# Turning all four quarters of the keys first, and letting a unit's scores accumulate in one bank

## The chip, the cores and the metric

The kernel runs on one core of one Trainium2 chip. A core has a matrix engine (TensorE, PE in the profile, with its weight loads as PEld), a vector engine (VectorE, DVE), a scalar engine (ScalarE, ACT), a general engine (GpSimd, POOL), a queue processor that here issues the large transfers (SyncE, SP), and 16 DMA engines that move data between the device's memory and the on-chip memory. The metric is the time of one execution on the device, in microseconds (us); less is better.

## What is computed

One decoding step of a windowed attention, gated by a small mixer, with residual:

```
xn = layernorm(x)                                    # x: 2 x 1 x 512
q  = (xn @ wq) as 32 heads of 128
k, v = the last 4096 positions of k_cache, v_cache   # 2 batches, 8 key heads
scores = q . k * 128**-0.5                           # 4 query heads share a key head
s  = (softmax(scores) @ v) as one row of 4096 @ wo
g  = silu(gmlp(xn, w_in, w_sp, b_sp, w_out))
out = x + s * g                                      # everything is float32
```

There is one query row for each batch and head, so nearly all of the work is reading: 16 windows of keys and 16 of values of 4096 x 128 numbers each, and the weights.

## The kernel before, in words

**Units.** The attention is cut into 8 units. A unit is one batch and two neighbouring key heads, so it has 8192 keys; units 0 to 3 are the first batch, 4 to 7 the second. The keys of a unit are one transfer of 4 MB that lays 64 keys (of 128 numbers) on each of the 128 partitions, and its values are another.

**The ring.** All large transfers go through `ring`, four slots of 4 MB each. `enqueue` gives each load the next slot in turn, and `advance` sends the loads, in the order in which they were enqueued, once the program has passed the place where their slot is given up. The loads are: `wq` (two slots), `w_in`, `w_out`, then keys and values by turns (k0, k1, v0, k2, v1, ... k7, v6, v7), and at the end `wo` in three slots: 16 blocks of its rows, then 8, then 4 and four single ones. They all stand in one queue of SP, and a load waits there for whoever still reads its slot.

**Order.** Every engine call passes through `InOrder`, so each engine runs its instructions in the order of the program text; the loop over the units near the end of the kernel sets it.

**Scores of a unit.** The product needs the head dimension on the partitions, so `turn(u, m)` (DVE) turns a quarter of the unit's keys, 16 keys of each partition, in blocks of 32 x 32 into `kt`. `shares(u, m)` then makes four products on PE, one for each quarter `dq` of the head dimension. The weights are the query, 128 x 32, laid out so that the rows of different groups of 32 partitions stay apart; each product writes 32 rows of one PSUM bank, `sh`. These are only shares: the four `dq` have still to be added. ACT copies the bank to `shs`, and `add_shares(u, m)`, a 128 x 128 product with zeros and ones (`add_dq`), adds them and puts them in the rows of bank `s` that belong to quarter `m`. So a unit has 16 products into `sh`, four copies and four products into `s`.

**Softmax and values of a unit.** `share_max` (DVE and one small product into `mo`) finds the maximum over a unit's keys and from it the shift `nb`; `probs` (ACT) takes the exponential of `s` with that shift into `p`; `probs_t` turns it into `pT` (DVE); `values` makes 16 products of `pT` with the unit's values into the bank `acc`, where each writes 32 rows, four row groups in turn; `scale_out` (ACT) keeps the wanted parts as `o`; `collect` adds `o` into the bank `col`, in which all units of a batch meet. `weigh` makes one over the sums of the exponentials, `wd`, at the last unit of a batch. These steps of unit u-1 stand inside unit u's loop step.

**End.** `gather`, `scale_out(last)`, `divide` and `collect_last` make the row `oT`, which the output product needs: 28 blocks of `wo` go into the bank `part`, which ACT copies to `parts`; the last four go into `so`, where the four row groups of `parts` are added to them. Two DVE instructions with the gate and x follow, and the output's transfer.

Of the kernel before, what the change touches and what calls it, by code (L numbers as in the profile page):

```python
# [9 lines left out]
F32 = mybir.dt.float32  # L10
AF = mybir.ActivationFunctionType
ALU = mybir.AluOpType
AX = mybir.AxisListType

P = 128
HQ, DH = 32, 128
G = 4
# [4 lines left out]
def ap(t, offset, dims):  # L22

    return bass.AP(tensor=t.tensor, offset=t.offset + offset, ap=[list(t.ap[0])] + [list(d) for d in dims])
# [18 lines left out]
def kernel(  # L43
# [13 lines left out]
    nc = tc.nc  # L57
    pe, dve, act, sp = (InOrder(tc, e) for e in (nc.tensor, nc.vector, nc.scalar, nc.sync))
    B, _, D = x.shape
    _, HKV, SK, _ = k_cache.shape  # L60
    W = min(4096, max(256, SK // 4))
    REP = HQ // HKV
# [8 lines left out]
    JC = 512 // 32  # L71
    NCH = J // JC
    SLOT = J * DH
    BANKS = {"s": 2, "sh": 2, "acc": 2, "mo": 1, "col": 1}

    cst = ctx.enter_context(tc.tile_pool(name="cst", bufs=1))
# [15 lines left out]
    def advance(*slots):  # L92
        for n in slots:
            free[n] = True
        while queue and all(free[n] for n in queue[0][1]):
            load, at = queue.pop(0)
            for n in at:
                free[n] = False
            load(ring[:, at[0] * SLOT : (at[-1] + 1) * SLOT], at[0])

    def const(name, *shape):
        return cst.tile([P, *shape], F32, tag=name, name=name)

    def bank(name, tag):
        return ps.tile([P, 512], F32, tag=tag, name=name, bufs=BANKS[tag])

# [33 lines left out]
    units = []  # L140
    for n in range(NU):
        u = Unit()
        u.n, u.kt, u.shs, u.slot = n, {}, {}, {}
        u.b, u.w = divmod(n, NU // B)
        units.append(u)

# [34 lines left out]
    nc.gpsimd.memset(hT, 0.0)  # L181
    x4 = const("x4", DC)
    nc.gpsimd.memset(x4, 0.0)
    add_dq = const("add_dq", NCH - 1 + P)
    nc.gpsimd.memset(add_dq, 0.0)
    sel = const("sel", 56)
    nc.gpsimd.memset(sel, 0.0)
    sel4 = const("sel4", 3 + 32)
# [62 lines left out]
    nc.gpsimd.tensor_mul(perm, ap(rowm, 0, [[1, 32], [0, G]]), ap(grpm, 0, [[0, 32], [1, G]]))  # L251
    perm = perm.rearrange("p h e -> p (h e)")
    for a in range(2):
        nc.gpsimd.tensor_copy(
            ap(add_dq, NCH - 1 + 16 * a, [[32, G], [4, REP]]),
            rowm[:, 16 * a : 16 * a + 16].rearrange("p (g h) -> p g h", g=G),
        )
    am = const("am", 2)
    dve.tensor_reduce(am, rowm.rearrange("p (a x) -> p a x", a=2), axis=AX.X, op=ALU.add)
    negm = const("negm", 2)  # L260
# [14 lines left out]
                    start=(k == 0), stop=(k == KT - 1),  # L275
                )
    advance(0, 1)
    qT = sb.tile([P, 1024], F32, tag="qT", name="qT", bufs=1)
    for r in range(2):
        dve.transpose(qT[:, 512 * r : 512 * r + 512], pq[r])  # L280
    qm = const("qm", 2 * B * 64)
# [12 lines left out]
    def q_of(u, dq):  # L294
        return ap(qbd, (u.n * 4 + dq) * 32, [[1, 32]])
# [52 lines left out]
    def spread_quarters(dst, shares, start=True, stop=True):  # L348
        for g in range(G):
            pe.matmul(  # L350
                dst[32 * g : 32 * g + 32, :], rowm, shares[:, g * DC : (g + 1) * DC], start=start, stop=stop,
            )
# [3 lines left out]
        g = j % G  # L356
        pe.matmul(yp[32 * g : 32 * g + 32, :], hT[:, j, :], wout[:, j, :], start=(j < G), stop=(j >= FT - G))
    advance(3)
    ys = sb.tile([P, D], F32, tag="shs", name="ys")
    act.activation(ys, yp, AF.Copy)  # L360
    y = bank("yq", "mo")[:, :DC]
    spread_quarters(y, ys)
    gate = const("gate", DC)
    dve.tensor_scalar(gate, y, -1.0, 80.0, op0=ALU.mult, op1=ALU.min)
    act.activation(gate, gate, AF.Exp)
    dve.tensor_scalar_add(gate, gate, 1.0)
    dve.reciprocal(gate, gate)
    dve.tensor_mul(gate, gate, y)


    def turn(u, m):

        u.kt[m] = sb.tile([P, JC, DH], F32, tag="kt", name=f"kt{u.n}_{m}", bufs=3)
        dve.transpose(
            u.kt[m].rearrange("p j d -> p (j d)"), u.k[:, JC * m : JC * m + JC, :].rearrange("p j d -> p (j d)")
        )

    def shares(u, m):

        u.sh = bank(f"sh{u.n}_{m}", "sh")  # L380
        for dq in range(4):
            pe.matmul(
                u.sh[32 * dq : 32 * dq + 32, :], q_of(u, dq), u.kt[m][:, :, 32 * dq : 32 * dq + 32],
                start=True, stop=True,
            )
        u.shs[m] = sb.tile([P, 512], F32, tag="shs", name=f"shs{u.n}_{m}")
        act.activation(u.shs[m], u.sh, AF.Copy)

    def add_shares(u, m):

        if m == 0:
            u.s = bank(f"s{u.n}", "s")
        pe.matmul(u.s, add_dq[:, NCH - 1 - m : NCH - 1 - m + P], u.shs[m], start=(m == 0), stop=(m == NCH - 1))

    def share_max(u):
        m2 = sb.tile([P, 2], F32, tag="m2", name=f"m2_{u.n}")
        dve.tensor_reduce(m2, ap(u.s, 0, [[1, 2], [2, 256]]), axis=AX.X, op=ALU.max)
        mg = sb.tile([P, 2, G * NCH], F32, tag="mg", name=f"mg{u.n}")
        dve.tensor_mul(mg, ap(m2, 0, [[1, 2], [0, G * NCH]]), spot.rearrange("p a g m -> p a (g m)"))
        u.mo = bank(f"mo{u.n}", "mo")  # L400
        dve.tensor_add(mg[:, 0], mg[:, 0], mg[:, 1])
        pe.matmul(u.mo[:, : G * NCH], same_r, mg[:, 0], start=True, stop=True)
        mx = sb.tile([P, 1], F32, tag="mx", name=f"mx{u.n}")
        dve.reduce_max(mx, u.mo[:, : G * NCH], axis=AX.X)
        u.nb = sb.tile([P, 2], F32, tag="nb", name=f"nb{u.n}")
        dve.scalar_tensor_tensor(u.nb, ap(mx, 0, [[0, 2]]), -SCALE, negm, op0=ALU.mult, op1=ALU.add)
# [3 lines left out]
    def probs(u):  # L410

        u.p = sb.tile([P, 512], F32, tag="p", name=f"p{u.n}")
        if u.w == 0:
            sums[u.b] = sb.tile([P, NU // B, 2], F32, tag="l", name=f"l{u.b}")
        for a in range(2):
            act.activation(
                ap(u.p, a, [[2, 256]]), ap(u.s, a, [[2, 256]]), AF.Exp,
                bias=u.nb[:, a : a + 1], scale=SCALE, accum_out=sums[u.b][:, u.w, a : a + 1],
            )
# [13 lines left out]
        pe.matmul(u.mo[:, 32:33], lr.rearrange("p w r e -> p (w r e)"), ones[:, 0:1], start=True, stop=True)  # L433
        dve.reciprocal(wd[:, u.b : u.b + 1], u.mo[:, 32:33])

    def values(u, part=0, parts=1):
        if part == 0:
            u.acc = bank(f"acc{u.n}", "acc")
        n = JC // parts
        for j in range(n * part, n * part + n):  # L440
            c = j % G
            pe.matmul(
                u.acc[32 * c : 32 * c + 32, :], u.pT[:, j, :], u.v[:, j : J : JC, :],
                start=(j < G), stop=(j >= JC - G),
            )

    def scale_out(u):
        u.o = sb.tile([P, 4, DH], F32, tag="o", name=f"o{u.n}")
        for jj in range(4):
            o, acc, m = u.o[:, jj, :], u.acc[:, jj * DH : (jj + 1) * DH], diag[:, jj : jj + 1]  # L450
            if u is units[-1] and jj >= 2:
                dve.tensor_scalar_mul(o, acc, m)
            else:
                act.activation(o, acc, AF.Copy, scale=m)
# [13 lines left out]
    def gather(b):  # L468

        hq = sb.tile([P, 32], F32, tag="hq", name=f"hq{b}")  # L470
        by_d = col[0][32 * b : 32 * b + 32, :].rearrange("p (j d) -> p d j", j=NCH)
        for e in range(4):
            dve.reduce_sum(hq[32 * e : 32 * e + 32, :], by_d[:, 32 * e : 32 * e + 32, :], axis=AX.X)
        t = bank(f"oT{b}", "acc")[:, :32]
        pe.matmul(t, perm, hq, start=True, stop=True)
        return t

    def divide(b, t, r=slice(0, P)):
        dve.tensor_scalar_mul(oT[r, :, 16 * b], t, wd[r, b : b + 1])
# [8 lines left out]
        dve.reduce_sum(ol[r, :], t.rearrange("p (j n) -> p n j", j=NCH), axis=AX.X)  # L488
        divide(u.b, ol[r, :], r)

    prev = old = None
    last = units[-1]
    for u in units:
        turn(u, 0)
        shares(u, 0)
        if old is not None and old.n == NU // B - 1:
            divide(0, gather(0))
        if prev is not None:
            share_max(prev)
            probs(prev)  # L500
        turn(u, 1)
        shares(u, 1)
        add_shares(u, 0)
        if prev is not None:
            probs_t(prev)
            weigh(prev)
            if u is not last:
                values(prev)
        for m in range(2, NCH):
            turn(u, m)  # L510
            shares(u, m)
            add_shares(u, m - 1)
        if u is not last and prev is not None:
            scale_out(prev)
        advance(u.slot["k"])
        add_shares(u, NCH - 1)
        if u is not last and prev is not None:
            advance(prev.slot["v"])
            collect(prev)
        old, prev = prev, u  # L520
    values(old, 0, 2)
    share_max(last)
    probs(last)
    values(old, 1, 2)
    advance(old.slot["v"])
    probs_t(last)
    weigh(last)
    scale_out(old)
    values(last, 0, 2)
    collect(old, old.w)  # L530
    early = slice(0, 32 * last.w)
    values(last, 1, 2)
    t = gather(last.b)
    scale_out(last)
    divide(last.b, t[early, :], early)
    collect_last(last)
# [4 lines left out]
    for n in range(EARLY):  # L541
        t, a = blocks[n]
        g = n % G
        pe.matmul(part[32 * g : 32 * g + 32, :], oT[:, n, :], t[:, a, :], start=(n < G), stop=(n >= EARLY - G))
    parts = sb.tile([P, D], F32, tag="shs", name="parts")
    act.activation(parts, part, AF.Copy)
    so = bank("so", "mo")[:, :DC]
    for n in range(EARLY, 32):
# [40 lines left out]
```

## Time and profile before

| | us |
|---|---|
| time, median of 3 runs | 217.53 |
| the three runs | 217.3, 217.53, 218.38 |
| span of the profiled execution, first to last instruction | 215.6 |
| PE busy | 144.9 (67%) |
| DVE busy | 107.1 (50%) |
| ACT busy | 43.7 (20%) |
| read from the device's memory | 89.40 MB, 415 GB/s over the span |

The profile is of one execution, and its span leaves out what lies around the first and last instruction: the median of the three runs is 1.93 us longer than the span. Times inside the span count from its start. A row of the timeline reads: start, duration, engine, line, operation, what is written and read, how many instructions are merged in it; and in brackets the engine's idle time ahead of it with what ended that. Nearly all rows name line 37, the helper that records every call, so the names of the tiles tell them apart. A float32 product shows as two instructions, so 16 products are x32.

### The profile page before, as it was taken

To read this page: it belongs to the slowest core of one execution; us is meant where nothing else is said; L and a number is where in the kernel's file an instruction comes from. 1 tells how busy PE (TensorE), PEld (TensorE's weight loads), DVE (VectorE), ACT (ScalarE), POOL (GpSimd) and SP (SyncE) were. 2 spreads that over 40 slices of the span, in tenths; PEclk is the share of its full clock that TensorE was granted. 3 is DMA by queue.
4 is the path that set the end of the run, shared out by engine and by line. 5 is a ranking of instruction groups with operands and counts; after the bars stand their busy time and mean duration, and the time that the engine had idled before them with its cause. 6 is when DMAs were issued, how large, how long until landed. Compare 5 with 4: busy or idle time off the path is not lost.

```text
span 215.6 us, 2181 instructions
## 1 busy us (share of the span) xinstructions
PE 144.9 (67%) x848; PEld 40.3 (19%) x848; DVE 107.1 (50%) x161; ACT 43.7 (20%) x108; POOL 4.2 (2%) x22
## 2 busy tenths in 40 slices
PE   0010787224595897699599499459949967987663
PEld 0010222100021222122122132112202211222311
DVE  1140025633995943953936663793585089233101
ACT  2030000331124115114303304130331231241001
POOL 6010000000000000000000000000000000000000
PEclk9999999658599699699799789859975996999998
DMA  9898999999999999999999999999999999999990
GB/s 389 390 389 389 431 423 459 435 438 421 450 395 474 395 453 419 444 432 425 439 404 450 419 444 429 432 432 419 444 413 447 425 432 444 425 435 404 410 376 33
DMA packets 3788, 89.52 MB, mean 415 GB/s; under 512 B 434, under 2 KB 450, under 8 KB 964
## 3 DMA queue, kind: packets, MB, share of 16 engines
q1 hardware_dynamic: 3772, 89.40, 96.9%
q8 instruction: 6, 0.10, 0.2%
q14 instruction: 2, 0.02, 0.0%
q10 hardware_dynamic: 8, 0.00, 0.0%
HBM read 89.40 MB, written 0.00 MB: 415 GB/s over the span
## 4 chain that ended last, share of the span: by engine, by line
DMA 41%; PE 39%; DVE 16%; ACT 2%; issue 2%; DVEq 0%
DMA ring<-in_A_wo_dram 20%; PE sh L37 11%; DMA ring<-in_A_k_cache_dram 11%; DVE kt L37 10%; DMA ring<-in_A_wq_dram 10%; PE s L37 10%; PE acc L37 7%; PE q_ps L37 4%; PE y L37 2%; PE z L37 1%; PE col L37 1%; PE mo L37 1%; DVE gate L37 1%; DVE u L37 1%; DVE qm L37 1%
## 5 line engine op out<-in xcount | busy, mean ns | idle before, releaser
L37 DVE STREAM_TRANSPOSE kt<-ring 128x2048 f32<-128x2048 f32 x32 | 72.2, 2286 | 24.9 <-DMA ring<-in_A_k_cache_dram 24.9
L37 PE MATMUL sh<-kt,qbd 128*32 128x512 f32 x256 | 43.6, 725 | 27.0 <-DVE kt L37 27.0
L37 ACT ACTIVATE shs<-sh 128x512 f32<-128x512 f32 x32 | 19.1, 597 | 99.4 <-PE sh L37 99.4
L37 PE MATMUL s<-shs,add_dq 128*128 128x512 f32 x64 | 39.0, 716 | 0.0
L37 PE MATMUL acc<-ring,pT 128*32 128x512 f32 x256 | 31.3, 614 | 0.0
L37 PEld LDWEIGHTS s<-shs,add_dq 128*128 128x128 f32 x64 | 11.0, 215 | 30.9 <-issue 26.5
L37 PEld LDWEIGHTS sh<-kt,qbd 128*32 128x32 f32 x256 | 7.0, 117 | 46.3 <-issue 38.3
L37 PE MATMUL q_ps<-ring,xnT 128*32 128x512 f32 x64 | 8.8, 713 | 7.6 <-DMA ring<-in_A_wq_dram 7.6
L37 PEld LDWEIGHTS acc<-ring,pT 128*32 128x32 f32 x256 | 7.8, 112 | 22.3 <-issue 17.6
L37 DVE TENSOR_REDUCE m<-s 128x2 f32<-128x512 f32 x8 | 5.4, 680 | 13.0 <-PE s L37 12.9
L37 PE MATMUL xnT_ps<-ident,xn 2*128 2x2 f32 x4 | 0.6, 252 | 14.5 <-DVE xn L37 14.5
L37 ACT ACTIVATE o<-acc,diag 128x128 f32<-128x128 f32 x30 | 8.6, 374 | 4.9 <-PE acc L37 4.9
L37 PE MATMUL part<-ring,oT 128*32 128x512 f32 x56 | 6.6, 597 | 3.5 <-DMA ring<-in_A_wo_dram 3.5
L37 ACT ACTIVATE p<-s,nb 128x256 f32<-128x256 f32 x16 | 7.6, 488 | 6.6 <-DVE nb L37 6.4
L37 DVE STREAM_TRANSPOSE qT<-q_ps 128x512 f32<-128x512 f32 x2 | 1.4, 717 | 14.4 <-PE q_ps L37 14.3
L37 PE MATMUL col<-o,sel 128*32 128x512 f32 x14 | 7.3, 601 | 0.0
L37 DVE TENSOR_TENSOR res<-so,gate 128x128 f32<-128x128 f32 x1 | 0.3, 292 | 11.5 <-PE so L37 11.5
L37 DVE STREAM_TRANSPOSE pT<-p 128x512 f32<-128x512 f32 x8 | 5.4, 674 | 1.2 <-ACT p L37 1.2
L37 PE MATMUL y<-ring,hT 128*32 128x512 f32 x14 | 3.3, 996 | 3.8 <-DVE hT L37 3.8
L37 ACT ACTIVATE zs<-z 128x448 f32<-128x448 f32 x1 | 0.5, 544 | 24.7 <-PE z L37 24.7
L37 ACT ACT_TABLE_LOAD x4 | 5.1, 1283 | 0.8 <-PEq L575 0.7
L37 PEld LDWEIGHTS q_ps<-ring,xnT 128*32 128x32 f32 x64 | 2.5, 130 | 13.1 <-issue 13.1
(114 smaller groups left out, 62.2 us busy)
## 6 DMA issues: line engine op xcount, KB each, us to landing
ring<-in_A_k_cache_dram SPq DMA_DIRECT2D x8, 4096.0 KB, 20.0
ring<-in_A_v_cache_dram SPq DMA_DIRECT2D x8, 4096.0 KB, 28.1
ring<-in_A_wo_dram SPq DMA_DIRECT2D x1, 4096.0 KB, 33.2
ring<-in_B_w_in_dram SPq DMA_DIRECT2D x1, 3584.0 KB, 17.1
ring<-in_A_wo_dram SPq DMA_DIRECT2D x1, 2048.0 KB
ring<-in_B_w_out_dram SPq DMA_DIRECT2D x1, 1792.0 KB, 21.0
ring<-in_A_wo_dram SPq DMA_DIRECT2D x1, 1024.0 KB
ring<-in_A_wo_dram SPq DMA_DIRECT2D x4, 256.0 KB, 17.6
```

Source lines behind the costliest of these rows:

```text
L37: return self.tc.keep_in_program_order(call(*args, **kwargs))
```

## The change

- A unit's four quarters are all turned before its scores are made; `kt` has five buffers in place of three, so that four stand ready.
- `scores` makes the same 16 products, now with the quarter `m` choosing the 32 rows and the four `dq` accumulating on them in PSUM. One copy to `shs` and one product with a permutation, `regroup`, put the rows in order. A unit has one copy and one 128 x 128 product where it had four of each.
- `share_max` is split: the maximum of the sums after the second turn, the shift (`shift`) and the exponentials after the third.
- `values` of the unit before stands behind the unit's scores: four products, then the permuting product, then twelve. `scale_out` and `collect` follow. This now holds for unit 7's loop step too, where before the values of unit 6 stood partly behind unit 7's maximum.
- The gate's last steps on DVE stand behind the second turn of unit 0. `yq` is one product and four copies of ACT in place of four products.

```diff
-    def shares(u, m):
-        u.sh = bank(f"sh{u.n}_{m}", "sh")
+    def scores(u):
+        u.sh = bank(f"sh{u.n}", "sh")
         for dq in range(4):
...
+            for m in range(NCH):
+                pe.matmul(
+                    u.sh[32 * m : 32 * m + 32, :], q_of(u, dq), u.kt[m][:, :, 32 * dq : 32 * dq + 32],
+                    start=(dq == 0), stop=(dq == 3),
+                )
+        u.shs = sb.tile([P, 512], F32, tag="shs", name=f"shs{u.n}", bufs=1)
+        act.activation(u.shs, u.sh, AF.Copy)
+    def by_group_of_keys(u):
+        u.s = bank(f"s{u.n}", "s")
+        pe.matmul(u.s, regroup, u.shs, start=True, stop=True)
...
     for u in units:
         turn(u, 0)
-        shares(u, 0)
...
+        turn(u, 1)
         if prev is not None:
             share_max(prev)
+        else:
+            form_gate()
+        turn(u, 2)
+        if prev is not None:
+            shift(prev)
             probs(prev)
...
+        turn(u, 3)
+        advance(u.slot["k"])
         if prev is not None:
             probs_t(prev)
             weigh(prev)
...
+        scores(u)
+        if prev is not None:
+            values(prev, range(G))
+        by_group_of_keys(u)
+        if prev is not None:
+            values(prev, range(G, JC))
             scale_out(prev)
...
+            collect(prev, prev.w if u is last else NU // B - 1)
+        prev = u
-    values(old, 0, 2)
     share_max(last)
+    shift(last)
     probs(last)
-    values(old, 1, 2)
-    advance(old.slot["v"])
     probs_t(last)
     weigh(last)
-    scale_out(old)
-    values(last, 0, 2)
-    collect(old, old.w)
     early = slice(0, 32 * last.w)
-    values(last, 1, 2)
+    values(last, range(8))
     t = gather(last.b)
+    values(last, range(8, JC))
     scale_out(last)
```

The first place is the end of unit 7 on PE. Before, from its last quarter's products on (`sh_3_882` and `s_866` are unit 7's scores, `acc_892` unit 6's values, `acc_941` unit 7's, `mo_905` its maximum and then its sums):

```order
L37 MATMUL sh_3_882<-kt_3_880,qbd 32x512 x4
L37 MATMUL s_866<-shs_2_877,add_dq 128x512
L37 MATMUL s_866<-shs_3_887,add_dq 128x512
L37 MATMUL acc_892<-ring,pT_868 32x512 x8
L37 MATMUL mo_905<-mg_903,same_r 128x16
L37 MATMUL acc_892<-ring,pT_868 32x512 x8
L37 MATMUL mo_905<-ones,lr_932 128x1
L37 MATMUL acc_941<-ring,pT_928 32x512 x8
L37 MATMUL col<-o_936,sel 32x512
L37 MATMUL acc_941<-ring,pT_928 32x512 x8
L37 MATMUL oT_964<-hq_959,perm 128x32
L37 MATMUL ol<-o_966,sel_89 32x128 x4
```

Now, from the last of the 16 score products on (`sh_776`, `s_800`: unit 7's scores; `acc_795`: unit 6's values; `acc_847`: unit 7's):

```order
L37 MATMUL sh_776<-kt_3_771,qbd 32x512
L37 MATMUL acc_795<-ring,pT_774 32x512 x4
L37 MATMUL s_800<-shs_793,regroup 128x512
L37 MATMUL acc_795<-ring,pT_774 32x512 x12
L37 MATMUL col<-o_814,sel 32x512
L37 MATMUL mo_829<-mg_827,same_r 128x16
L37 MATMUL mo_829<-ones,lr_843 128x1
L37 MATMUL acc_847<-ring,pT_839 32x512 x8
L37 MATMUL oT_861<-hq_856,perm 128x32
L37 MATMUL acc_847<-ring,pT_839 32x512 x8
L37 MATMUL ol<-o_871,sel_88 32x128 x4
```

The two small products into `mo` now follow each other with nothing between, all of unit 6's values and its `col` stand ahead of them, and the gathering product stands between the halves of unit 7's values.

The second place is DVE in unit 7, from its first turn to the maximum of its own scores. Before (`s_782` and `pT_868` are unit 6's):

```order
L37 STREAM_TRANSPOSE kt_0_834<-ring 128x2048
L37 TENSOR_REDUCE m_6_843<-s_782 128x2
L37 TENSOR_TENSOR mg_845<-m_6_843,spot 128x32
L37 TENSOR_TENSOR mg_845<-mg_845 128x16
L37 TENSOR_REDUCE mx_850<-mo_847 128x1
L37 SCALAR_TENSOR_TENSOR nb_852<-mx_850,negm 128x2
L37 STREAM_TRANSPOSE kt_1_857<-ring 128x2048
L37 STREAM_TRANSPOSE pT_868<-p_854 128x512
L37 STREAM_TRANSPOSE kt_2_870<-ring 128x2048
L37 STREAM_TRANSPOSE kt_3_880<-ring 128x2048
L37 TENSOR_REDUCE m_7_901<-s_866 128x2
```

Now (`s_728` and `pT_774` are unit 6's):

```order
L37 STREAM_TRANSPOSE kt_0_751<-ring 128x2048
L37 STREAM_TRANSPOSE kt_1_753<-ring 128x2048
L37 TENSOR_REDUCE m_6_755<-s_728 128x2
L37 TENSOR_TENSOR mg_757<-m_6_755,spot 128x32
L37 TENSOR_TENSOR mg_757<-mg_757 128x16
L37 STREAM_TRANSPOSE kt_2_762<-ring 128x2048
L37 TENSOR_REDUCE mx_764<-mo_759 128x1
L37 SCALAR_TENSOR_TENSOR nb_766<-mx_764,negm 128x2
L37 STREAM_TRANSPOSE kt_3_771<-ring 128x2048
L37 STREAM_TRANSPOSE pT_774<-p_768 128x512
L37 TENSOR_REDUCE m_7_825<-s_800 128x2
```

The work is the same; the turning of unit 6's exponentials moved from ahead of the third turn to behind the fourth, and the small product for the maximum now runs beside the third turn.

More of the change, by code (lines that the diff above doesn't have):

```diff
@@ L73 @@
     SLOT = J * DH
+    KTB = 5
     BANKS = {"s": 2, "sh": 2, "acc": 2, "mo": 1, "col": 1}
@@ L142 @@
         u = Unit()
-        u.n, u.kt, u.shs, u.slot = n, {}, {}, {}
+        u.n, u.kt, u.slot = n, {}, {}
         u.b, u.w = divmod(n, NU // B)
@@ L183 @@
     nc.gpsimd.memset(x4, 0.0)
-    add_dq = const("add_dq", NCH - 1 + P)
-    nc.gpsimd.memset(add_dq, 0.0)
+    regroup = const("regroup", G, 2, REP, NCH)
     sel = const("sel", 56)
@@ L253 @@
     for a in range(2):
[L254 to L257, printed above, removed]
+        nc.gpsimd.tensor_copy(regroup[:, :, a], ap(ident, 16 * a, [[4, G], [1, REP], [32, NCH]]))
+    regroup = regroup.rearrange("p g a h m -> p (g a h m)")
     am = const("am", 2)
@@ L277 @@
     advance(0, 1)
-    qT = sb.tile([P, 1024], F32, tag="qT", name="qT", bufs=1)
+    qT = sb.tile([P, JC, DH], F32, tag="kt", name="qT", bufs=KTB).rearrange("p j d -> p (j d)")
     for r in range(2):
@@ L358, with form_gate @@
     advance(3)
-    ys = sb.tile([P, D], F32, tag="shs", name="ys")
+    ys = sb.tile([P, D], F32, tag="shs", name="ys", bufs=1)
     act.activation(ys, yp, AF.Copy)
-    y = bank("yq", "mo")[:, :DC]
-    spread_quarters(y, ys)
-    gate = const("gate", DC)
[L364 to L368, printed above, removed]
+    yp = bank("yq", "mo")
+    pe.matmul(yp, same, ys, start=True, stop=True)
+    y = const("y", DC)
+    for g in range(G):
+        r = slice(32 * g, 32 * g + 32)
+        act.activation(y[r, :], yp[r, g * DC : (g + 1) * DC], AF.Copy)
+    gate = const("gate", DC)
+    def form_gate():
+        dve.tensor_scalar(gate, y, -1.0, 80.0, op0=ALU.mult, op1=ALU.min)
+        act.activation(gate, gate, AF.Exp)
+        dve.tensor_scalar_add(gate, gate, 1.0)
+        dve.reciprocal(gate, gate)
+        dve.tensor_mul(gate, gate, y)
     def turn(u, m):
-        u.kt[m] = sb.tile([P, JC, DH], F32, tag="kt", name=f"kt{u.n}_{m}", bufs=3)
+        u.kt[m] = sb.tile([P, JC, DH], F32, tag="kt", name=f"kt{u.n}_{m}", bufs=KTB)
         dve.transpose(
@@ L376, in turn @@
         )
-    def shares(u, m):
-        u.sh = bank(f"sh{u.n}_{m}", "sh")
+    def scores(u):
+        u.sh = bank(f"sh{u.n}", "sh")
         for dq in range(4):
[L382 to L393, printed above, removed]
+            for m in range(NCH):
[8 more added lines that the diff above has]
+        pe.matmul(u.s, regroup, u.shs, start=True, stop=True)
     def share_max(u):
@@ L402, in share_max, with shift @@
         pe.matmul(u.mo[:, : G * NCH], same_r, mg[:, 0], start=True, stop=True)
+    def shift(u):
         mx = sb.tile([P, 1], F32, tag="mx", name=f"mx{u.n}")
@@ L434, in weigh, with values @@
         dve.reciprocal(wd[:, u.b : u.b + 1], u.mo[:, 32:33])
-    def values(u, part=0, parts=1):
-        if part == 0:
+    def values(u, js=range(JC)):
+        if js[0] == 0:
             u.acc = bank(f"acc{u.n}", "acc")
-        n = JC // parts
-        for j in range(n * part, n * part + n):
+        for j in js:
             c = j % G
@@ L447, in scale_out @@
     def scale_out(u):
-        u.o = sb.tile([P, 4, DH], F32, tag="o", name=f"o{u.n}")
+        u.o = sb.tile([P, 4, DH], F32, tag="o", name=f"o{u.n}", bufs=1)
         for jj in range(4):
@@ L489, in collect_last @@
         divide(u.b, ol[r, :], r)
-    prev = old = None
     last = units[-1]
+    prev = None
     for u in units:
         turn(u, 0)
-        shares(u, 0)
-        if old is not None and old.n == NU // B - 1:
+        if u.n == NU // B + 1:
             divide(0, gather(0))
+        turn(u, 1)
         if prev is not None:
             share_max(prev)
+        else:
[3 more added lines that the diff above has]
+            shift(prev)
             probs(prev)
-        turn(u, 1)
-        shares(u, 1)
-        add_shares(u, 0)
+        turn(u, 3)
+        advance(u.slot["k"])
         if prev is not None:
@@ L506 @@
             weigh(prev)
[L507 to L513, printed above, removed]
+        scores(u)
[4 more added lines that the diff above has]
+            values(prev, range(G, JC))
             scale_out(prev)
-        advance(u.slot["k"])
-        add_shares(u, NCH - 1)
-        if u is not last and prev is not None:
             advance(prev.slot["v"])
-            collect(prev)
-        old, prev = prev, u
-    values(old, 0, 2)
+            collect(prev, prev.w if u is last else NU // B - 1)
+        prev = u
     share_max(last)
+    shift(last)
     probs(last)
-    values(old, 1, 2)
-    advance(old.slot["v"])
     probs_t(last)
     weigh(last)
-    scale_out(old)
-    values(last, 0, 2)
-    collect(old, old.w)
     early = slice(0, 32 * last.w)
-    values(last, 1, 2)
+    values(last, range(8))
     t = gather(last.b)
+    values(last, range(8, JC))
     scale_out(last)
@@ L544 @@
         pe.matmul(part[32 * g : 32 * g + 32, :], oT[:, n, :], t[:, a, :], start=(n < G), stop=(n >= EARLY - G))
-    parts = sb.tile([P, D], F32, tag="shs", name="parts")
+    parts = sb.tile([P, D], F32, tag="shs", name="parts", bufs=1)
     act.activation(parts, part, AF.Copy)
```

## The prediction

> **What bounds the kernel now.** I read the page's slices first, then the chain that ended last, then the timeline of the queue and of the last unit. The slices, 40 to the span, 5.39 us each:
>
> ```profile
> DMA  9898999999999999999999999999999999999990
> GB/s 389 390 389 389 431 423 459 435 438 421 450 395 474 395 453 419 444 432 425 439 404 450 419 444 429 432 432 419 444 413 447 425 432 444 425 435 404 410 376 33
> ```
>
> The DMA engines are full from the fifth slice to the last but one, at 404 to 474 GB/s but for two slices at 395 and the last full one at 376. No engine can bring a byte sooner. The chain ends the same way:
>
> ```profile
> 201.98 9.97 DMA ring<-in_A_wo_dram
> 211.99 0.47 PE so L37 x8
> ```
>
> The last block of `wo` is there at 211.99, PE adds it until 212.46, and DVE's two instructions and the output's transfer take the remaining 3.1 us. So this is a stream that never stops, with a short tail. Compute counts in two cases only: it gives up a slot too late and the stream starves, or it isn't done with `oT` when `wo` has landed.
>
> The stream has room:
>
> ```profile
> 109.70 0.54 SPq L37 DMA_DIRECT2D ring<-in_A_k_cache_dram  x1
> 114.57 2.31 DVE L37 STREAM_TRANSPOSE kt<-ring 128x2048 f32<-128x2048 f32 x1 [4.89 <-DMA ring<-in_A_k_cache_dram]
> 133.91 2.31 DVE L37 STREAM_TRANSPOSE kt<-ring 128x2048 f32<-128x2048 f32 x1 [3.62 <-DMA ring<-in_A_k_cache_dram]
> 172.86 2.31 DVE L37 STREAM_TRANSPOSE kt<-ring 128x2048 f32<-128x2048 f32 x1 [7.98 <-DMA ring<-in_A_k_cache_dram]
> ```
>
> Unit 4's keys landed at 114.57 and unit 5's at 133.91: two transfers take 19.3 us, one 9.7. Unit 5's keys were issued at 109.70; ahead of them stood the rest of unit 4's keys and unit 3's values, until about 124.2. They could have been issued 14 us later. Unit 7's keys land at 172.86.
>
> **The tail before**, from the timeline:
>
> ```profile
> 175.10 0.65 DVE L37 TENSOR_REDUCE m<-s 128x2 f32<-128x512 f32 x1
> 177.04 2.30 DVE L37 STREAM_TRANSPOSE kt<-ring 128x2048 f32<-128x2048 f32 x1
> 179.86 4.46 DVE L37 STREAM_TRANSPOSE kt<-ring 128x2048 f32<-128x2048 f32 x2
> 186.18 1.98 PE L37 MATMUL s<-shs,add_dq 128*128 128x512 f32 x4
> 188.20 0.69 DVE L37 TENSOR_REDUCE m<-s 128x2 f32<-128x512 f32 x1 [3.88 <-PE s L37]
> 190.27 1.92 PE L37 MATMUL acc<-ring,pT 128*32 128x512 f32 x16
> 190.38 0.17 DVE L37 TENSOR_REDUCE mx<-mo 128x1 f32<-128x16 f32 x1 [1.05 <-PE mo L37]
> 191.91 0.71 DVE L37 STREAM_TRANSPOSE pT<-p 128x512 f32<-128x512 f32 x1 [1.16 <-ACT p L37]
> 192.26 1.15 ACT L37 ACTIVATE o<-acc,diag 128x128 f32<-128x128 f32 x4 [0.39 <-PE acc L37]
> 193.04 0.38 PE L37 MATMUL mo<-ones,lr 128*128 128x1 f32 x2 [0.85 <-DVE lr L37]
> 197.77 0.41 PE L37 MATMUL oT<-hq,perm 128*128 128x32 f32 x2
> 197.91 0.63 ACT L37 ACTIVATE o<-acc,diag 128x128 f32<-128x128 f32 x2 [4.50 <-PE acc L37]
> 200.73 0.25 DVE L37 TENSOR_SCALAR oT<-ol,wd 32x32 f32<-32x32 f32 x1
> 202.09 3.64 PE L37 MATMUL part<-ring,oT 128*32 128x512 f32 x32 [1.74 <-DMA ring<-in_A_wo_dram]
> 206.91 1.92 PE L37 MATMUL part<-ring,oT 128*32 128x512 f32 x16 [1.17 <-DMA ring<-in_A_wo_dram]
> 209.41 1.07 PE L37 MATMUL part<-ring,oT 128*32 128x512 f32 x8 [0.58 <-DMA ring<-in_A_wo_dram]
> 210.60 0.60 ACT L37 ACTIVATE parts<-part 128x512 f32<-128x512 f32 x1 [12.06 <-PE part L37]
> 211.50 0.92 PE L37 MATMUL so<-ring,oT 128*32 128x128 f32 x16
> ```
>
> `oT` is ready at 200.98, 1 us ahead of `wo`, and PE then waits three times for data (1.74, 1.17, 0.58). How late may `oT` be? The 28 products into `part`, without waits, take 6.0 us (a group of 16 each 3.44, so 0.215 a product), 0.2 more until the bank is written; the copy 0.6 and 0.1; the quarters' sum and the last two blocks about 0.9. That is 7.8 us; to end at 212.46 `oT` has to be ready by about **204.7**. Each later us is a us of the time.
>
> **The clock.** PE's clock decides this tail. The windows below (columns: width, then PE, PEld, DVE, ACT, POOL busy with counts, granted clock, DMA share, GB/s) lie on the grid of 3.41 us on which every change of clock in this trace falls:
>
> ```profile
> 135.45:138.86 3.41, 1.40 (x10) 0.48 (x10) 2.79 (x8) 0.60 (x1) 0.00 (x0) 1.00 1.00 432
> 138.86:142.27 3.41, 0.61 (x2) 0.50 (x2) 2.64 (x5) 1.03 (x4) 0.00 (x0) 0.50 0.94 404
> 142.27:145.69 3.42, 3.16 (x10) 0.73 (x10) 3.42 (x4) 0.60 (x1) 0.00 (x0) 0.50 1.07 460
> 145.69:149.10 3.41, 3.41 (x29) 0.94 (x32) 1.68 (x1) 0.00 (x0) 0.00 (x0) 1.00 1.00 432
> 159.34:162.75 3.41, 2.70 (x9) 0.73 (x10) 3.41 (x4) 0.60 (x1) 0.00 (x0) 0.50 1.05 452
> 162.75:166.17 3.42, 3.42 (x14) 0.60 (x16) 2.13 (x1) 0.00 (x0) 0.00 (x0) 0.50 1.02 441
> 200.30:203.71 3.41, 1.68 (x17) 0.65 (x20) 0.55 (x2) 0.00 (x0) 0.00 (x0) 1.00 0.91 385
> 203.71:207.13 3.42, 2.25 (x24) 0.63 (x20) 0.00 (x0) 0.00 (x0) 0.00 (x0) 1.00 0.97 405
> ```
>
> A window with 1.40 us of PE work at full clock is followed by one at half; after 1.68 us the clock stays. At half clock a window with 3.16 us (93%) brings the full clock back, one with 2.70 us (79%) doesn't. What half clock costs:
>
> ```profile
> 136.37 1.06 PE L37 MATMUL sh<-kt,qbd 128*32 128x512 f32 x8 [1.32 <-DVE kt L37]
> 139.15 0.61 PE L37 MATMUL mo<-mg,same_r 128*128 128x16 f32 x2 [1.38 <-DVE mg L37]
> 142.53 1.93 PE L37 MATMUL sh<-kt,qbd 128*32 128x512 f32 x8 [2.77 <-DVE kt L37]
> ```
>
> Four score products take 1.06 at full and 1.93 at half: 0.215 and 0.43 a product.
>
> **The change, part by part.** (1) Per unit three 128 x 128 products and three copies go. That is 24 x about 1 us of PE and 24 x 0.6 of ACT, in the loop wholly beside the stream: worth 0. (2) Slots: a unit's keys are turned 10.3 us after they land (worked out in 5), well inside the room of 14 us. The values of the unit before are given up later than now, behind the unit's scores: about 20 us after the keys landed (192.8 less 172.86 in 5). The load for that slot has to stand in the queue when the keys two units on have landed, 38.6 us after. Both 0. (3) The gate and `yq` move beside unit 0's turns, whose keys' slot is needed at about 74: 0. Cover gone would show as an empty DMA slice. (4) `regroup` for `add_dq` on POOL, at the start: 0.
>
> (5) **The end of unit 7.** Its keys still land at 172.86. Four turns of 2.23 (half of 4.46, and 0.08 more for the last's end) and the maximum's five small instructions between them (1.94 from 175.10 to 177.04, less 0.5 of it that was waiting for PE) end the fourth turn at 183.2; before it was 184.32. But of the scores only three products are done by then, where three quarters were. Thirteen remain: 2.8 us at full clock, 5.6 at half. PE has had only single products since about 176, so it starts at half clock; full returns at the end of the first window with over about 85% work, after 3 to 6 us. Scores end at 187.7 to 189, middle 188.3. Four products of unit 6's values hide the copy (0.9), the permuting product takes 1.0: `s` is ready at 190.2, against 188.16.
>
> From here on nothing overlaps that overlapped before. Unit 6's twelve products end at 192.8 (2.6), `o` of ACT at 194.0 (0.07 and 1.15), `col`, one product, at 195.0 (half of 1.98), and only then comes the small product for the maximum: 195.4, where before the maximum was read at 190.38. The way from there to the next small product, the sums, takes 2.7 us as before (190.38 to 193.04): 198.1. Before, half of unit 6's values filled it; now PE stands idle. So between 192.8 and 198.1 PE has 1.4 us of work in 5.3. Wherever the grid lies, one whole window of 3.41 falls (nearly) into this hole, with 1.4 us or less, and the clock halves. It returns after one window if that is full, else after two. Unit 7's 16 products and the gathering one are 3.8 us at full clock (198.4 to 202.2); with 3.4 us of half clock they lose 1.4 to 1.7, with more up to 3. I take 2.0: 204.2. From there to `oT` it is 3.2 us (197.8 to 200.98): 207.4.
>
> **The sum.** `oT` at 207.4 against a limit of 204.7 is +2.7; a further window of low work stands between 204.2 and 207.5 (only the products for `ol`), which can halve the clock for the start of `part`; that is 1.7 us more where it falls so, about one time in five: +0.3. Together **+3.0**: span 218.6. The median stood 1.93 above the profiled span, so **220.5**. With the grid shifted through its 3.41 us the same sum gives +2.0 to +3.7.
>
> **The rivals.** *The clock stays up in the hole.* Then unit 7's values end at 202.2 and `oT` is ready at 205.4: +0.7, or 0 if the scores too ran at full clock (`s` at 188.5). 217.5 to 218.2, so not slower. It decides at a work share between 0.41 and 0.49 of a window. Against it: the hole's share is 0.41 at most and mostly single instructions; for it: the grid of another execution is not this one's. 0.14. The Trainium skill, "TensorE: Matmul & The Clock Gate", section "Why this matters for your kernels", asks for no PE gaps over about 3 us. By that rule the gaps here, 1.3 and 2.7 us, would leave the clock up and this rival would hold. The trace disagrees: the gaps of 1.32 and 1.38 us around 136.37 were enough.
>
> *The row groups don't overlap when they accumulate in one bank.* Sixteen products one after the other at 0.86 (four at 0.215) are 13.8 us for 3.4; unit 7 ends 10 us later than worked out above, 228 to 231, and the loop comes near its 19.3 us a unit. Against it: `acc` does just this, 16 products in four row groups of one bank, at 0.215 each (190.27: eight in 1.92). 0.02. The Trainium skill, "TensorEngine Tiling (Array Packing)", section "Restrictions and Gotchas", says that different row tiles cannot access the same PSUM bank at the same time. That would give this rival; the row at 190.27 doesn't bear it out for these 128 x 32 products.
>
> *The stream gets shorter.* With slots free earlier and less work on chip the transfers could run nearer to the 474 GB/s of the best slice. Against it: the rate doesn't follow the load; slices with idle engines are no better. If it took 1% off 190 us: 216 to 216.5. 0.04.
>
> **How the numbers follow.** Forecast 0.80 (219.2 to 221.6), clock up 0.14, serial groups 0.02, shorter stream 0.04. A measurement tells about 0.5%, 1.1 us, from no change. Slower by more takes the forecast and the serial case, 0.80 with a little of the forecast's lower edge lost; same has the second, 0.16; faster 0.04. The range reaches from inside the second case, 218.0, to the top of the first, 221.7.
>
> **What would show it.** Right: unit 7's keys at about 173; `s` of unit 7 at 190; half clock between 196 and 203; `oT` near 207; the first `part` product not waiting for DMA, and the 28 in one row; the last block landed at 212 and waiting for PE. Wrong: an empty DMA slice between 22 and 200 (slots), full clock from 190 on, or `oT` before 205.

## The result, and the profile after

| | before | after |
|---|---|---|
| median, us (6 runs each) | 217.53 | 219.61 |
| lowest and highest run | 217.30 to 218.44 | 219.27 to 220.12 |
| ratio to before, 95% interval | | 1.009 [1.007, 1.0109] |
| span of the profiled execution | 215.6 | 218.1 |
| PE busy, ACT busy | 144.9, 43.7 | 134.6, 31.1 |
| `oT` ready, in the span | 200.98 | 207.05 |

The kernel became 2.1 us slower, 0.9%, although TensorE is busy for 10.3 us less and ScalarE for 12.6 us less. The slices of the page of the changed kernel:

```profile
DMA  9889999999999999999999998999999999999950
GB/s 385 385 385 411 442 407 453 448 409 458 409 451 415 451 415 448 409 457 403 463 400 463 403 463 385 476 391 475 388 463 403 463 403 457 406 457 394 407 224 1
```

The transfers are as dense as before; they end in the last slice but one, and the last slice is empty. What ends the kernel is another thing now. The end of the chain of waits:

```profile
207.11 6.26 PE part L37 x56
214.04 0.91 PE so L37 x24
```

Before, the last long piece of this chain was a transfer of `wo`. Now the 28 products into `part` run in one row of 6.26 us, with no wait for a transfer between them, and the last blocks of `wo` wait for TensorE. The way there, from the timeline:

```profile
178.72 3.60 PE L37 MATMUL sh<-kt,qbd 128*32 128x512 f32 x6
182.88 3.19 PE L37 MATMUL sh<-kt,qbd 128*32 128x512 f32 x25 [0.56 <-DVE kt L37]
188.34 2.78 PE L37 MATMUL acc<-ring,pT 128*32 128x512 f32 x24
188.45 0.69 DVE L37 TENSOR_REDUCE m<-s 128x2 f32<-128x512 f32 x1 [5.04 <-PE s L37]
192.45 1.04 PE L37 MATMUL col<-o,sel 128*32 128x512 f32 x2 [1.32 <-ACT o L37]
193.42 0.40 PE L37 MATMUL mo<-mg,same_r 128*128 128x16 f32 x2
196.45 0.59 PE L37 MATMUL mo<-ones,lr 128*128 128x1 f32 x2 [2.63 <-DVE lr L37]
196.96 3.64 PE L37 MATMUL acc<-ring,pT 128*32 128x512 f32 x16
201.10 2.74 PE L37 MATMUL acc<-ring,pT 128*32 128x512 f32 x16
206.80 0.25 DVE L37 TENSOR_SCALAR oT<-ol,wd 32x32 f32<-32x32 f32 x1
213.39 0.60 ACT L37 ACTIVATE parts<-part 128x512 f32<-128x512 f32 x1 [8.78 <-PE part L37]
```

The maximum of unit 7's scores starts at 188.45, only 0.25 us later than before (188.20). The delay comes behind it. PE waits 1.32 us ahead of `col` and 2.63 us ahead of the product for the sums, and then unit 7's values go slowly: 16 instructions take 3.64 us at 196.96, where 32 took that at full clock (202.09, in the kernel before). The windows on the clock's grid (columns as in the prediction) say why:

```profile
189.15:192.56 3.41, 2.09 (x21) 0.51 (x14) 0.37 (x2) 1.14 (x4) 0.00 (x0) 1.00 0.96 413
192.56:195.98 3.42, 1.26 (x4) 0.32 (x3) 1.00 (x4) 1.02 (x4) 0.00 (x0) 1.00 0.93 402
195.98:199.39 3.41, 2.94 (x14) 1.09 (x18) 1.68 (x8) 0.00 (x0) 0.00 (x0) 0.50 1.00 432
199.39:202.80 3.41, 3.41 (x18) 0.90 (x14) 0.00 (x0) 0.00 (x0) 0.00 (x0) 0.50 0.94 400
202.80:206.20 3.40, 1.85 (x20) 0.92 (x12) 0.78 (x3) 0.62 (x2) 0.00 (x0) 1.00 0.98 414
```

The second window has 1.26 us of work, and the clock is halved for the next two, just when unit 7's values run. The wait of 1.32 us, from 191.12 to 192.45, lies in the first window, which has 2.09 us of work and doesn't halve the clock. The second window begins behind it: its idle time is 2.16 us of the other wait.

### The profile page after: what moved, and what is told of

The parts are those of the page before. It is cut to its first block, busy times and chain, and to the rows that moved or that the text cites. A ratio compares the mean times of both kernels' runs of the same rounds, so it can differ in the third digit from the quotient of the medians.

```text
span 218.1 us, 2001 instructions
## 1 busy us (share of the span) xinstructions
PE 134.6 (62%) x794; PEld 36.2 (17%) x794; DVE 106.8 (49%) x161; ACT 31.1 (14%) x88; POOL 4.2 (2%) x21
## 4 chain that ended last, share of the span: by engine, by line
PE 35%; DMA 31%; DVE 25%; ACT 5%; issue 2%; ACTq 0%; DVEq 0%
DMA ring<-in_A_k_cache_dram 21%; DVE kt L37 16%; DMA ring<-in_A_wq_dram 10%; PE sh L37 9%; PE acc L37 8%; PE q_ps L37 5%; PE part L37 3%; PE z L37 2%; PE s L37 2%; ACT o L37 2%; PE y L37 2%; PE col L37 1%; DVE m L37 1%; PE mo L37 1%; DVE gate L37 1%
## 5 line engine op out<-in xcount | busy, mean ns | idle before, releaser
L37 PE MATMUL sh<-kt,qbd 128*32 128x512 f32 x256 | 52.3, 733 | 12.3 <-DVE kt L37 11.5
L37 PE MATMUL acc<-ring,pT 128*32 128x512 f32 x256 | 38.1, 638 | 0.0
L37 PEld LDWEIGHTS sh<-kt,qbd 128*32 128x32 f32 x256 | 10.3, 128 | 47.9 <-DVE kt L37 22.7
L37 PE MATMUL q_ps<-ring,xnT 128*32 128x512 f32 x64 | 10.0, 795 | 7.4 <-DMA ring<-in_A_wq_dram 7.4
L37 PEld LDWEIGHTS acc<-ring,pT 128*32 128x32 f32 x256 | 8.9, 114 | 20.7 <-issue 20.6
L37 ACT ACTIVATE shs<-sh 128x512 f32<-128x512 f32 x8 | 4.8, 597 | 52.0 <-PE sh L37 52.0
L37 PE MATMUL mo<-mg,same_r 128*128 128x16 f32 x16 | 3.8, 313 | 13.1 <-DVE mg L37 13.1
L37 PE MATMUL s<-shs,regroup 128*128 128x512 f32 x16 | 9.0, 643 | 0.8 <-ACT shs L37 0.8
L37 PEld LDWEIGHTS mo<-mg,same_r 128*128 128x128 f32 x16 | 3.0, 234 | 19.2 <-DVE mg L37 13.7
L37 PE MATMUL mo<-ones,lr 128*128 128x1 f32 x4 | 1.2, 363 | 7.7 <-DVE lr L37 7.7
```

The source lines that it names most:

```text
L37: return self.tc.keep_in_program_order(call(*args, **kwargs))
```

## The experiments

The theory: the whole loss lies in the order at the end of unit 7. Part of it is that steps now follow each other that ran side by side; the rest is that a wait of TensorE there halves its clock. The rivals: the order alone; the loop, the slots or the stream; the new way of making the scores.

| kernel | median, us | lowest to highest (runs) | ratio to before | `oT` ready |
|---|---|---|---|---|
| both waits filled | 217.48 | 217.42 to 219.77 (12) | 1.0013 [0.9988, 1.0037] | 204.5 |
| old order at the end | 217.45 | 217.31 to 217.63 (12) | 0.999 [0.9978, 1.0002] | 202.3 |
| before, with the new end | 220.42 | 220.04 to 221.42 (6) | 1.0127 [1.0103, 1.015] | 207.6 |
| fourth quarter first | 222.1 | 221.34 to 223.0 (6) | 1.0205 [1.0174, 1.0235] | 209.0 |
| only the first wait filled | 219.43 | 218.66 to 219.87 (6) | 1.0078 [1.0058, 1.0098] | 206.6 |
| only the second wait filled | 217.52 | 217.35 to 219.77 (12) | 1.0013 [0.999, 1.0036] | 204.4 |
| a third stretch filled too | 217.43 | 217.32 to 217.79 (12) | 0.9995 [0.9987, 1.0004] | 204.2 |

The last column is from each profile: the end of the last instruction that writes `oT`.

### Filling both waits

Extra products that nobody reads keep TensorE at work; nothing else moves.

```diff
+    spare = []
+
+    def fill(count):
+        if not spare:
+            spare.append(bank("fill", "sh"))
+        for i in range(count):
+            m = i % NCH
+            pe.matmul(spare[0][32 * m : 32 * m + 32, :], q_of(last, 0), last.kt[m][:, :, :32], start=True, stop=True)
...
             scale_out(prev)
             advance(prev.slot["v"])
+            if u is last:
+                fill(4)
...
     share_max(last)
+    fill(12)
     shift(last)
```

> The changed kernel with 16 extra products that nobody reads, in the two stretches in which TensorE waits at the end of unit 7: 4 while ACT scales unit 6's output (1.32 us of waiting), 12 between the small products for the maximum and for the sums (2.6 us). No other instruction moves. Theory (the end of unit 7 is late, and most of that is half clock): the clock stays at 1.00 from 183 on, unit 7's 16 value products take 3.8 us with the gathering one in place of 6.9, oT is ready near 204 and the time is 217.5 to 218.0. Rival A (the order alone, the clock is a bystander): the same row of waits, 219.3 to 219.9. Rival B (the loss is in the stream or the loop): 219.6, too.

Measured: 217.48, the time of before. From its profile, unit 7's maximum, values and `oT`, and the window in which the changed kernel had 1.26 us of work:

```profile
188.87 0.69 DVE L37 TENSOR_REDUCE m<-s 128x2 f32<-128x512 f32 x1 [5.03 <-PE s L37]
197.19 1.92 PE L37 MATMUL acc<-ring,pT 128*32 128x512 f32 x16
199.39 1.92 PE L37 MATMUL acc<-ring,pT 128*32 128x512 f32 x16
204.26 0.26 DVE L37 TENSOR_SCALAR oT<-ol,wd 32x32 f32<-32x32 f32 x1
```
```profile
192.44:195.85 3.41, 2.98 (x20) 0.98 (x24) 0.44 (x3) 1.41 (x6) 0.00 (x0) 1.00 1.03 442
```

The same 16 instructions take 1.92 us in place of 3.64, and `oT` is ready at 204.5 in place of 207.05. More work on TensorE made the kernel 2.1 us faster. So the clock is no bystander. Without the half clock the change still makes `oT` 3.5 us later (204.5 against 200.98), and the slack that the prediction worked out, until 204.7, just covers that; the 2.5 us of half clock come on top and are what the time shows. The maximum of unit 7's scores starts a little differently in each profile, so the two are best told apart by the way from there to `oT`: 12.8 us before (188.20 to 200.98), 15.7 with both waits filled (188.87 to 204.52), 18.6 in the changed kernel (188.45 to 207.05). On that way the order costs 2.9 us and the half clock another 2.9. Three of the twelve runs took 218.9 to 219.8 (the expectation of the last experiment says four); the third stretch below bears on them.

### The old order at the end, with the new scores

```diff
-        if prev is not None:
+        if prev is not None and u is not last:
             values(prev, range(G, JC))
             scale_out(prev)
...
+    values(old, range(G, 10))
     share_max(last)
+    values(old, range(10, JC))
+    advance(old.slot["v"])
     shift(last)
     probs(last)
     probs_t(last)
     weigh(last)
+    scale_out(old)
...
     values(last, range(8))
+    collect(old, old.w)
+    values(last, range(8, JC))
     t = gather(last.b)
-    values(last, range(8, JC))
```

> The changed kernel, but after unit 7's scores the order of before: the product for unit 7's maximum stands between unit 6's value products (4 and 6 ahead, 6 behind), unit 6's scaling and its col behind unit 7's exponentials. Turning first, accumulating in one bank, one copy and one permuting product stay in all units. Theory: the whole loss is in this order at the end; no stretch of low TensorE work, full clock, oT ready at 200.5 to 202, the last block of wo ends the kernel again: 217.3 to 217.8. Rival B (loop, slots or start cost something): stays over 218.5.

Measured: 217.45. The loop, the slots, the start, the accumulation and the single copy stay as changed in all eight units, so together they cost nothing that can be measured, and the 11 us of TensorE work and 13 of ScalarE that they save bring nothing either. `oT` is 1.3 us later than before, but nearly all of that lies ahead of the maximum, which starts at 189.44; from there to `oT` it is 12.8 us, as before. `part` waits for its transfers again:

```profile
189.44 0.69 DVE L37 TENSOR_REDUCE m<-s 128x2 f32<-128x512 f32 x1 [5.60 <-PE s L37]
202.02 0.26 DVE L37 TENSOR_SCALAR oT<-ol,wd 32x32 f32<-32x32 f32 x1
202.33 3.64 PE L37 MATMUL part<-ring,oT 128*32 128x512 f32 x32 [0.68 <-DVE oT L37]
207.10 1.92 PE L37 MATMUL part<-ring,oT 128*32 128x512 f32 x16 [1.13 <-DMA ring<-in_A_wo_dram]
209.64 1.06 PE L37 MATMUL part<-ring,oT 128*32 128x512 f32 x8 [0.62 <-DMA ring<-in_A_wo_dram]
```

### The kernel before with the new order at its end

```diff
-    values(old, 0, 2)
+    values(old)
+    scale_out(old)
+    advance(old.slot["v"])
+    collect(old, old.w)
     share_max(last)
     probs(last)
-    values(old, 1, 2)
-    advance(old.slot["v"])
     probs_t(last)
     weigh(last)
-    scale_out(old)
-    values(last, 0, 2)
-    collect(old, old.w)
     early = slice(0, 32 * last.w)
-    values(last, 1, 2)
+    values(last, 0, 2)
     t = gather(last.b)
+    values(last, 1, 2)
```

> The kernel before with nothing changed but the end: all of unit 6's value products, its scaling and its col ahead of the product for unit 7's maximum, and the gathering product between the halves of unit 7's values. Scores are made and added as before. Theory: the same loss without any of the new scores: half clock from about 196 on, oT near 207, 219.2 to 220.4. Rival B or a rival that blames the accumulation or the late scores: 217.5.

Measured: 220.42. Without any of the new scores the loss is there, and its place is the same:

```profile
197.10 0.58 PE L37 MATMUL mo<-ones,lr 128*128 128x1 f32 x2 [2.63 <-DVE lr L37]
197.61 3.64 PE L37 MATMUL acc<-ring,pT 128*32 128x512 f32 x16
207.39 0.25 DVE L37 TENSOR_SCALAR oT<-ol,wd 32x32 f32<-32x32 f32 x1
```

With that the rival falls that blames the accumulation or the late scores. It is 0.8 us slower than the changed kernel: there four of unit 6's value products stand ahead of `s`, beside the copy, here all 16 stand behind it, and the product for the maximum starts at 194.07 in place of 193.42.

### The fourth quarter first

In the changed kernel three products of a unit, one for each of the first three quarters, can run ahead of the fourth turn. Here none can.

```diff
         for dq in range(4):
-            for m in range(NCH):
+            for m in (3, 0, 1, 2):
```

> The changed kernel with the quarters of the score products taken in the order 3, 0, 1, 2: every product now waits for the fourth turn, so none runs alone ahead of it. Theory now (after the result): the three lone products of unit 7 took as long as whole groups of four, 1.92 us each at half clock, filled a window and brought full clock back just before the other thirteen. Without them all 16 start at half clock: scores end 1.5 to 2.5 us later than 186.5, and the time is 220.8 to 222.0. Rival (full clock at 182.3 was the grid's luck, or lone products cost nothing): 219.3 to 220.0.

Measured: 222.1, 0.1 above the theory's span and far from the rival's. The 16 score products start with the fourth turn and run at half clock until 187.34; the maximum starts 2.3 us later than in the changed kernel:

```profile
183.12 5.71 PE L37 MATMUL sh<-kt,qbd 128*32 128x512 f32 x32 [4.39 <-DVE kt L37]
190.78 0.69 DVE L37 TENSOR_REDUCE m<-s 128x2 f32<-128x512 f32 x1 [7.21 <-PE s L37]
```

So the three early products of the changed kernel do a service. In its profile two of them run side by side and the third alone, and each time that takes 1.92 us, as long as a group of four:

```profile
178.72 1.92 PE L37 MATMUL sh<-kt,qbd 128*32 128x512 f32 x4
180.40 1.92 PE L37 MATMUL sh<-kt,qbd 128*32 128x512 f32 x2
```

Its window with them, between its neighbours:

```profile
175.50:178.91 3.41, 0.73 (x4) 0.69 (x6) 3.34 (x5) 0.00 (x0) 0.00 (x0) 0.50 0.96 413
178.91:182.32 3.41, 3.41 (x6) 0.18 (x2) 3.38 (x4) 1.03 (x4) 0.00 (x0) 0.50 1.01 432
182.32:185.74 3.42, 2.86 (x28) 0.94 (x32) 1.09 (x2) 0.00 (x0) 0.00 (x0) 1.00 1.05 450
```

Six instructions, three products, fill 3.41 us, and full clock is back for the other thirteen. How much of them it catches depends on where the windows lie: in the five profiles of the other kernels with this order of scores the same 25 instructions took 3.19 to 3.82 us, against 3.19 here.

### One wait at a time

These two kernels are the first experiment with one of its two `fill` calls left out: only `fill(4)`, ahead of `col`, or only `fill(12)`, ahead of the sums.

> The filled kernel with only the first stretch filled: 4 unread products while ACT scales unit 6's output. TensorE then has one wait left, 2.6 us from the maximum's product to the sums'. Theory (a window of 3.41 us with too little work halves the clock, wherever it lies): a window that covers about 1.9 us or more of that wait has under 45% work, so the clock halves in some 60% of the runs: two groups, one near 217.5, one near 219.5, the median at 218.5 to 219.8. Rival (a wait has to last over 3 us, or both waits are needed): full clock always, all runs at 217.4 to 218.0.

> The filled kernel with only the second stretch filled: 12 unread products between the maximum's and the sums' product. The wait left is 1.3 us, ahead of unit 6's col, and no window there has under 60% work. Theory: as with both filled, median 217.4 to 218.0 (with some runs above 218.5, as there, where something else halves the clock). Rival (both waits together do it, half each): between, 218.3 to 218.8.

Measured: 219.43 with the second wait left open, 217.52 with the first left open. In the profiles the 2.6 us wait alone halves the clock, and the 1.3 us wait alone doesn't. The expectation of two groups was a miss: all six runs with the 2.6 us wait took 218.66 to 219.87. Its profile has the window, with the whole wait in it:

```profile
194.75:198.16 3.41, 0.78 (x7) 0.46 (x10) 1.69 (x7) 1.02 (x4) 0.00 (x0) 1.00 0.98 423
198.16:201.57 3.41, 3.41 (x22) 1.04 (x18) 0.99 (x4) 0.00 (x0) 0.00 (x0) 0.50 0.95 405
```

Whether the grid lay like this in all six or the bound of about 45% work is higher than I took it stays open. With the first wait left open three of twelve runs took 219.06 to 219.77, as many as with both filled.

### A third stretch

Four more unread products behind unit 7's values, ahead of the products for `ol`.

```diff
     values(last, range(8, JC))
+    fill(4)
     scale_out(last)
```

> The kernel with both waits filled, and 4 more unread products behind unit 7's values, while ACT and DVE scale them (1.54 us of waiting ahead of the products for ol). With both waits filled 4 of 12 runs took 218.9 to 219.8 where the others took 217.4 to 217.8. Theory: these are the runs in which a window falls between unit 7's values and the first block of wo (1.0 us of work in 3.4) and halves the clock for the first part products; with 4 more products there every such window has over 55% work, and all runs take 217.4 to 218.0. Rival (in those runs unit 7's scores ran at half clock, or it is something else): the share of runs above 218.5 stays near one in three.

Measured: all twelve runs took 217.32 to 217.79. The upper group of the two kernels with the 2.6 us wait filled, three runs in twelve each, is gone, as the theory had it. At that rate, six in 24, twelve runs without one would come about by chance once in thirty. No trace caught one of those upper runs, so that their clock was halved at `part` is inferred, not seen. Their mean granted clock, 0.866 to 0.875 against 0.869 to 0.881 in the other runs, leans that way and doesn't decide it.

## Why the prediction was right

The direction, the place and the mechanism hold; the time, 219.61, lies in the range, 0.9 us under the 220.5 forecast. Step by step:

| step | forecast | profile after |
|---|---|---|
| fourth turn ends | 183.2 | 182.83 |
| unit 7's `s` ready | 190.2 | 188.4 |
| unit 6's values end | 192.8 | 191.1 |
| `col` ends | 195.0 | 193.5 |
| product for the sums starts | 198.1 | 196.45 |
| unit 7's values end | 204.2 | 203.84 |
| `oT` ready | 207.4 | 207.05 |
| limit for `oT` | 204.7 | |
| from `oT` to the last product into `so` | 7.8 | 7.85 (207.05 to 214.90) |

**Edits priced at 0** (fewer products and copies, slots, gate, `regroup`): right, by the kernel with the old order at its end, 0.999 [0.9978, 1.0002].

**The limit of 204.7** was right: the filled kernel has `oT` at 204.5 and the time of before. The four profiles with a later `oT` (206.6, 207.05, 207.6 and 209.0) have spans 2.1, 2.5, 3.2 and 4.5 us longer than before, each 0.1 to 0.3 more than `oT` is past the limit.

**Scores of unit 7** were mis-sized, 1.8 us too late, 0.4 of it from the fourth turn. The step was "Thirteen remain: 2.8 us at full clock, 5.6 at half", with PE starting at half clock. The thirteen ran at full clock (182.88, 25 of their 26 instructions in 3.19 us), because a product of 32 rows alone takes as long as a group of four: the early ones, which I took for too little work to bring the clock back, filled a window.

**Half clock in unit 7's values** was mis-sized the other way: "I take 2.0" for a loss that was 2.8. From 196.96 to 203.84 are 6.9 us; the filled kernel takes 4.1 (from 197.19 to 199.39 and 1.92 more), where the sum had 3.8. The clock came back after two windows, not one, as the 2.94 us of work in the first were not enough. The two errors, and smaller ones of some 0.6 us together, nearly cancel, so that `oT` came 0.35 us from the forecast is in part luck.

**The further window**, "about one time in five: +0.3", did not strike in the profiled run (202.80 to 206.20 kept full clock with 1.85 us of work). With the third stretch filled, the runs that looked like it disappeared; no profile shows one.

**What is left** of the difference between +3.0 and +2.1 is this 0.3, the 0.35 of `oT`, and the profiled execution itself: it took 219.93, 0.3 above its median.

**Two slips of 0.1 us** change nothing: the turns and the five small instructions add up to 183.3, where the prediction writes 183.2, and it gives the top of the forecast as 221.6 and as 221.7.

**The rivals.** The clock did not stay up. The Trainium skill, "TensorE: Matmul & The Clock Gate", section "Why this matters for your kernels", sets about 3 us as the gap that matters; a wait of 2.63 us alone cost 1.8 us of time here (219.43 against 217.65 in the same comparison), so the measurement decides against the figure. The row groups did overlap while accumulating in one bank: 25 of the 26 instructions of 13 products in 3.19 us. The sentence of the Trainium skill on row tiles, which the prediction cites, does not bear on this rival: these products all read 128 partitions and differ in the rows of the bank that they write. The stream got no shorter: in the kernel with the old order at its end, which waits for it, the last transfer ended at 212.1, and before at 211.9. The removed work lay wholly beside it.

## What to carry to other kernels

Where a transfer stream bounds a kernel, find the latest time at which each result may be ready and look at the last unit: a loop step that is right seven times, hidden behind the stream, can be wrong the eighth, where nothing follows to fill its waits. In such a tail do not price a wait of TensorE by its length alone; add up the work in every window of the clock's length around it, as half clock behind a wait can cost more than the wait. The cheapest test of a clock theory is to fill the waits with products that nobody reads: if more work makes the kernel faster, the clock it was.

## What the runs showed of the hardware

- A single product of 128 x 32 by 512 takes as long as four that go to different row groups in turn: 1.92 us at half clock for one (180.40) and for two (178.72), and 1.93 for four (142.53 before). While it runs alone it counts as work for the clock: a window of 3.41 us with only three such products in it brought full clock back.
- A window of 3.42 us with 1.26 us of work, 2.16 us of a wait of 2.63 in it, halved the clock for 6.8 us (195.98 to 202.80). With that wait as the only one left (0.78 us of work in the window) the clock was halved for one window, 3.41 us. A wait of 1.32 us did not halve it, in a window with 2.09 us of work (189.15 to 192.56).
- 2.94 us of work in a window at half clock (195.98 to 199.39) did not bring full clock back, while 2.89 us had done so in the kernel before (46.70 to 50.11). Near 85% the busy time of the profile doesn't tell which way the clock goes.
